# Attention beside a gated MLP on one core: the first token block's normalisation and gate/up matmuls rearranged, and the V tile's row cut from 136 to 129 elements

## The chip, the cores and the metric

The kernel runs on one core of a Trainium2 chip. The metric is the device time of one execution in microseconds (us). A core has a matmul engine (TensorE, PE in the profile; its weight loads are PEld), a vector engine (DVE), a scalar engine for activations (ACT), a general engine (POOL) and an engine that here only issues transfers (SP). They run side by side and wait for each other through semaphores; each works through its own instructions in order.

## The reference

```python
xn = layernorm(A_x)                               # 2048 x 512
q  = (xn @ wq) as 32 heads of 2048 x 128
p  = softmax(q @ k_cache^T * 128**-0.5)           # 2048 keys a head
s  = concat over heads(p @ v_cache) @ wo          # 2048 x 512
gate, up = xn @ W_gate, xn @ W_up                 # 2048 x 1792
g  = silu((relu(gate) * up) @ W_down)             # 2048 x 512
out = A_x + s * g
```

Everything is bf16 in memory; sums of products are float32.

## The kernel before, in words

The whole kernel is one program whose engine orders are written out by hand: each helper appends instructions to several engines' streams and returns a token (a semaphore and its count) that a later instruction waits for.

The 2048 tokens are 4 blocks (Q = 0 to 3) of 512 tokens, each of 4 tiles of 128. The first stage is the gated MLP. For each block the normalised tokens must stand transposed in `xnT` (features on the partitions). `emit_gate_up(Q)` (L462) makes 14 chunks (fc) of 128 hidden features: 4 matmuls of 512 columns with W_gate (L481) and 4 with W_up (L485), each group into one PSUM bank. Two banks are a slot of a ring of three slots (`ring_acquire`, L303), ps_r. ACT takes the relu of the gate bank (L448), DVE multiplies by the up bank (L454), which frees the slot. `emit_down(Q)` (L491) multiplies by W_down. While block 0's chunks run, DVE and ACT make the layer norm coefficients of the later blocks (`ln_task`, L416), POOL normalises those tiles (L340) and SP transposes them by DMA (L432).

Block 0 has no earlier work to hide behind; its path is the head, `head_ln` (L367). DVE takes the statistics of the tiles (L315, L320), ACT a square root (L326), DVE the reciprocal and a product (L331, L334) for tiles 0 and 1 together, and later for 2 and 3. All four tiles are normalised on DVE (`ln_norm`, L340), transposed on PE (`head_transpose`, L353) into PSUM tile ps_acc, and copied to `xnT` by ACT, the last by DVE (L359). PE runs 12 matmuls of zeros before (L365, `warm_mm`) and 3 more after the first two tiles' transposes. Then `emit_half(0, ...)` (L391) computes gate and up of the first three chunks (HFC = 3) for the first 256 tokens alone, as matmuls of 256 columns (L407), while tiles 2 and 3 are still being normalised; `emit_half(1, ...)` does the other 256 tokens. `emit_gate_up(0)` then only finishes these chunks, and goes on at full width from chunk 3.

The gate and up weights come in three pieces each, cut at the chunks FCS = 0, 3, 8, 14 (`load_w`, L220), all issued by SP; of the four x tiles of block 0 SP and ACT issue two each.

The second stage is attention, head by head, with blocks of 512 queries: scores (L625, 512 columns), exponential on ACT (L635), and the product with V (PV, L722): the exponentials are the stationary operand, and the moving operand is a row of `V_sb`, 128 values and a column of twos that gives the softmax denominator, so 129 columns. There are 8192 of these matmuls. `V_sb` has room for VS = 136 elements a row, of which 129 are used. V is loaded by SP, one transfer a head (L261), two heads ahead. `emit_norm_block` (L644) normalises a finished block and has SP transpose it by DMA (L661); the output projection of a group of four heads (L579) waits for the group's transposes.

Of the kernel before, what the change touches and what calls it, by code (L numbers as in the profile page):

```python
# [5 lines left out]
BF16 = mybir.dt.bfloat16  # L6
F32 = mybir.dt.float32
ALU = mybir.AluOpType
ACTF = mybir.ActivationFunctionType
# [42 lines left out]
def bass_recurrent_scan__mha_block_cached__glu_gated_reglu__prompt_kernel(  # L52
# [12 lines left out]
    _, S, D = A_x.shape  # L65
# [8 lines left out]
    DC = D // 128  # L74
# [13 lines left out]
    NBLK = H * QB  # L88
    TOTP = NBLK * NP
    VW = Dh + 1  # L90
    VS = Dh + 8
    TPG = 16 * G * QB

    x2 = A_x[0]
# [10 lines left out]
    with ExitStack() as es:  # L105
        _cnt = [0]

        def S_(shape, dt, name):
            _cnt[0] += 1
            return es.enter_context(nc.sbuf_tensor(f"{name}_{_cnt[0]}", shape, dt))  # L110
# [15 lines left out]
        ident = S_([128, 128], BF16, "ident")  # L126
        eps_sb = S_([128, 1], F32, "eps_sb")
        KT_sb = [S_([128, Sk], BF16, "KT_sb") for _ in range(2)]
        V_sb = [S_([128, KT, VS], BF16, "V_sb") for _ in range(2)]
        QT_sb = [S_([128, S], BF16, "QT_sb") for _ in range(2)]  # L130
        Wq_sb = [S_([128, DC, Dh], BF16, "Wq_sb") for _ in range(2)]
        Wo_sb = [S_([128, G, D], BF16, "Wo_sb") for _ in range(2)]
# [65 lines left out]
        with nc.Block() as block:  # L198

            @block.tensor  # L200
            def _(_pe_eng):
# [10 lines left out]
                for b in range(2):  # L212
                    tok_pool = sem_pool.sig(pool.memset(V_sb[b][:, :, Dh:VW], 2.0))

                FCS = [0, min(3, FC), min(8, FC), FC]
                HFC = 3
                wg_src = B_W_gate.rearrange("(c p) f -> p c f", p=128)
                wu_src = B_W_up.rearrange("(c p) f -> p c f", p=128)

# [18 lines left out]
                load_x0(sp, 2)  # L238
                load_x0(act, 3)
                load_w(sp, Wg_sb, wg_src, sem_wg, 0)  # L240
                load_w(sp, Wu_sb, wu_src, sem_wu, 0)
                load_w(sp, Wg_sb, wg_src, sem_wg, 1)
                load_w(sp, Wu_sb, wu_src, sem_wu, 1)
                if QB > 1:
# [98 lines left out]
                xt_ready = {Q: [] for Q in range(QB)}  # L343

                def head_transpose(n, ntok, eng, sem):
                    tp_ps = acc_bf[n % 2]
                    _wait(pe, acc_free[n % 2])
                    if n == 0:
                        _wait(pe, tok_pool)
                    _wait(pe, ntok)  # L350
                    ins = None
                    for c in range(DC):
                        ins = pe.transpose(tp_ps[:, c * 128:(c + 1) * 128],  # L353
                                           xn_sb[:, n, c * 128:(c + 1) * 128], ident[:])
                    ptok = sem_tp.sig(ins)
                    src = tp_ps[:, 0:DC * 128].rearrange("p (c q) -> p c q", c=DC)
                    _wait(eng, ptok)
                    copy = act.copy if eng is act else dve.tensor_copy
                    ctok = sem.sig(copy(xnT[:, :, n * 128:(n + 1) * 128], src))  # L359
                    xt_ready[0].append(ctok)  # L360
                    acc_free[n % 2] = ctok

                def warm_mm(k):
                    for _i in range(k):
                        pe.matmul(ps_r[:, 2 * NSLOT - 1, 0:D], warm[:, 0:128], warm[:], start=True, stop=True)  # L365

                def head_ln():  # L367
                    st = ln_stats(0)
                    st = ln_stats(1)
                    sq01 = ln_aggr([0, 1], st)  # L370
                    st = ln_stats(2)
                    c01 = ln_coef([0, 1], sq01)
                    n0 = ln_norm(dve, sem_ln4, 0, c01)
                    n1 = ln_norm(dve, sem_ln4, 1, c01)
                    head_transpose(0, n0, act, sem_xa)
                    head_transpose(1, n1, act, sem_xa)
                    warm_mm(3)
                    st = ln_stats(3)
                    sq23 = ln_aggr([2, 3], st)
                    emit_half(0, range(HFC - 1), xt_ready[0][0:2])  # L380
                    c23 = ln_coef([2, 3], sq23)
                    n2 = ln_norm(dve, sem_ln4, 2, c23)
                    n3 = ln_norm(dve, sem_ln4, 3, c23)
                    head_transpose(2, n2, act, sem_xa)
                    head_transpose(3, n3, dve, sem_xt)
                    emit_half(0, range(HFC - 1, HFC), [])
                    emit_half(1, range(HFC), xt_ready[0][2:4])

                half_slots = []

                def emit_half(k, fcs, toks):  # L391
                    hs = slice(k * 256, (k + 1) * 256)
                    for fc in fcs:
                        fs = slice(fc * 128, (fc + 1) * 128)
                        if k == 0:
                            if fc == 0:
                                pe.wait_ge(sem_wg[0].h, 16)
                            half_slots.append(ring_acquire())
                        if fc == 0:
                            _wait_all(pe, toks)  # L400
                        s = half_slots[fc]
                        for i, W in enumerate((Wg_sb, Wu_sb)):
                            if k == 0 and fc == 0 and i == 1:
                                pe.wait_ge(sem_wu[0].h, 16)
                            ins = None
                            for c in range(DC):
                                ins = pe.matmul(ps_r[:, 2 * s + i, hs], W[:, c, fs], xnT[:, c, hs],  # L407
                                                start=(c == 0), stop=(c == DC - 1))
                            if k == 1:
                                half_tok[(fc, i)] = (sem_gate if i == 0 else sem_gu).sig(ins)  # L410

                half_tok = {}

                ln_hold = {}

# [23 lines left out]
                sig_free = [None, None]  # L439
                hT_free = [None, None]  # L440

                def finish_gate_up(Q, fc, s, gtok, gu_tok):
                    par = Q % 2
                    gb = 2 * s
                    gk = fc % NSLOT
                    _wait(act, gtok)
                    _wait(act, gr_free[gk])
                    rtok = sem_relu.sig(act.activation(gr_sb[gk][:], ps_r[:, gb, :], ACTF.Relu))  # L448
                    _wait(dve, gu_tok)
                    _wait(dve, rtok)  # L450
                    if fc == 0:
                        _wait(dve, hT_free[par])
                    h_tok = sem_h.sig(
                        dve.tensor_tensor(hT[par][:, fc, :], gr_sb[gk][:], ps_r[:, gb + 1, :], ALU.mult)  # L454
                    )
                    gr_free[gk] = h_tok
                    ring_tok[s] = [rtok, h_tok]
                    if Q == 0:
                        ln_task(fc)
                    return h_tok  # L460

                def emit_gate_up(Q):  # L462
                    qs = slice(Q * NQ, (Q + 1) * NQ)
                    h_tok = None
                    for fc in range(FC):
                        fs = slice(fc * 128, (fc + 1) * 128)
                        if Q == 0 and fc < HFC:
                            s = half_slots[fc]
                            finish_gate_up(Q, fc, s, half_tok[(fc, 0)], half_tok[(fc, 1)])
                            continue  # L470
                        s = ring_acquire()
                        gb = 2 * s
                        if fc == 0:
                            _wait_all(pe, xt_ready[Q])
                        if Q == 0 and fc in FCS:
                            k = FCS.index(fc)
                            pe.wait_ge(sem_wg[k].h, 16)
                            pe.wait_ge(sem_wu[k].h, 16)
                        ins = None
                        for c in range(DC):  # L480
                            ins = pe.matmul(ps_r[:, gb, :], Wg_sb[:, c, fs], xnT[:, c, qs],  # L481
                                            start=(c == 0), stop=(c == DC - 1))
                        gtok = sem_gate.sig(ins)
                        for c in range(DC):
                            ins = pe.matmul(ps_r[:, gb + 1, :], Wu_sb[:, c, fs], xnT[:, c, qs],  # L485
                                            start=(c == 0), stop=(c == DC - 1))
                        gu_tok = sem_gu.sig(ins)
                        h_tok = finish_gate_up(Q, fc, s, gtok, gu_tok)
                    return h_tok

                def emit_down(Q, h_last_tok):  # L491
# [27 lines left out]

                assert DC == 4 and FC >= 4 * (QB - 1) + 1  # L520
                _wait(pe, warm_w)
                warm_mm(12)
                head_ln()
                for Q in range(QB):
                    hlast = emit_gate_up(Q)
                    if Q < QB - 1:
                        emit_down(Q, hlast)
# [177 lines left out]
                def emit_PV_tile(gp, tt):  # L705
# [11 lines left out]
                    for j in range(4):  # L717
                        bank = j // 2
                        if t == 0 and j % 2 == 0:
                            _wait(pe, norm_tok[b - 1][bank] if b >= 1 else acc_free[bank])  # L720
                        o_ap = ps_acc[:, bank, (j % 2) * 256:(j % 2) * 256 + VW]
                        ins = pe.matmul(o_ap, PT[pb][:, tt, j * 128:(j + 1) * 128], V_sb[vb][:, t, 0:VW],  # L722
                                        start=(t == 0 and j % 2 == 0), stop=(t == KT - 1 and j % 2 == 1))
                        if b == NBLK - 1 and t == KT - 1 and j == 1:
                            tx = sem_pv.sig(ins)
# [138 lines left out]
```

## Time and profile before

| | us |
|---|---|
| median of three runs | 1287.91 (1287.7 to 1288.04) |
| profiled execution, its own time | 1287.7 |
| its span, first to last instruction | 1285.8 |
| ACT's exponentials, L635, x1024 | 952.5 busy, 1054 ns each |
| scores, L625, 512 columns, x2048 | 754.1 busy, 379 ns each |
| gate and up at full width, L481 and L485, x212 each | 54.4 busy each, 379 ns each |
| V loads, L261, x32 | 512 KB each, 4.5 to landing |

The page gives an engine's busy time and, for a group of instructions, line, engine, operation, tiles, count, busy time and the mean duration of one. Matmuls are pipelined: the 379 ns of one with 512 columns is from its start to its modelled end, while the next starts 216 ns after it; so sums for PE go by the distances of starts, not by the durations. The chain of work that ended last follows back, from the last instruction, what each step waited for.

### The profile page before, as it was taken

To read this page: it belongs to the slowest core of one execution; us is meant where nothing else is said; L and a number is where in the kernel's file an instruction comes from. 1 tells how busy PE (TensorE), PEld (TensorE's weight loads), DVE (VectorE), ACT (ScalarE), POOL (GpSimd) and SP (SyncE) were. 2 spreads that over 40 slices of the span, in tenths; PEclk is the share of its full clock that TensorE was granted. 3 is DMA by queue.
4 is the path that set the end of the run, shared out by engine and by line. 5 is a ranking of instruction groups with operands and counts; after the bars stand their busy time and mean duration, and the time that the engine had idled before them with its cause. 6 is when DMAs were issued, how large, how long until landed. Compare 5 with 4: busy or idle time off the path is not lost.

```text
span 1285.8 us, 26847 instructions
## 1 busy us (share of the span) xinstructions
PE 1279.2 (99%) x11995; PEld 834.8 (65%) x11995; DVE 380.0 (30%) x682; ACT 1001.4 (78%) x1109; POOL 10.0 (1%) x21
## 2 busy tenths in 40 slices
PE   9999999999999999999999999999999999999998
PEld 4444476666666666666666666666666666666665
DVE  6333311112222222222222222222222222234456
ACT  3322399998888888888888888888888888888884
POOL 2000000000000000000000000000000000000000
PEclk9999999999999999999999999999999999999999
DMA  9500123232222332232322322332223321233302
GB/s 266 111 1 1 21 36 67 57 54 40 36 51 50 71 54 50 54 71 51 54 46 37 60 47 53 55 67 55 54 51 71 55 34 38 50 67 55 50 14 74
DMA packets 238801, 71.60 MB, mean 56 GB/s; under 512 B 225632, under 2 KB 238688, under 8 KB 238688
## 3 DMA queue, kind: packets, MB, share of 16 engines
q1 hardware_dynamic: 238400, 69.63, 27.8%
q8 instruction: 96, 1.57, 0.5%
q10 hardware_dynamic: 288, 0.26, 0.1%
q14 instruction: 17, 0.14, 0.0%
HBM read 32.77 MB, written 2.10 MB: 27 GB/s over the span
## 4 chain that ended last, share of the span: by engine, by line
PE 99%; DVE 1%; issue 0%; DMA 0%; ACT 0%
PE ps_acc L722 36%; PE ps_r L625 34%; PE ps_r L558 9%; PE ps_r L579 8%; PE ps_acc L504 4%; PE ps_r L485 4%; PE ps_r L481 4%; PE ps_r L759 1%; DVE fin_tmp L767 0%; PE ps_r L407 0%; DMA x_sb<-in_A_x_dram 0%; DVE stats L315 0%; ACT xnT L359 0%; PE ps_acc L353 0%; DVE x_sb L772 0%
## 5 line engine op out<-in xcount | busy, mean ns | idle before, releaser
L635 ACT ACTIVATE PT<-ps_r 128x1024 bf16<-128x1024 f32 x1024 | 952.5, 1054 | 167.7 <-PE ps_r L625 167.7
L722 PEld LDWEIGHTS ps_acc<-V_sb,PT 128*128 128x128 bf16 x8192 | 621.1, 98 | 241.7 <-ACT PT L635 3.5
L722 PE MATMUL ps_acc<-V_sb,PT 128*128 128x129 bf16 x8192 | 776.5, 220 | 0.0
L625 PE MATMUL ps_r<-QT_sb,KT_sb 128*128 128x512 bf16 x2048 | 754.1, 379 | 0.0
L652 DVE RECIPROCAL rz_sb<-ps_acc 128x4 f32<-128x4 f32 x127 | 23.3, 183 | 729.6 <-PE ps_acc L722 729.6
L625 PEld LDWEIGHTS ps_r<-QT_sb,KT_sb 128*128 128x128 bf16 x2048 | 195.0, 98 | 1.1 <-DVE QT_sb L569 0.4
L558 PE MATMUL ps_r<-xnT,Wq_sb 128*128 128x512 bf16 x512 | 130.9, 379 | 0.0
L579 PE MATMUL ps_r<-Wo_sb,OT_store 128*128 128x512 bf16 x448 | 114.6, 379 | 0.0
L569 DVE CAST QT_sb<-ps_r 128x512 bf16<-128x512 f32 x128 | 88.5, 692 | 48.1 <-PE ps_r L558 48.1
L558 PEld LDWEIGHTS ps_r<-xnT,Wq_sb 128*128 128x128 bf16 x512 | 49.9, 97 | 60.7 <-ACT PT L635 27.1
L655 DVE TENSOR_TENSOR Onorm<-ps_acc,rz_sb 128x512 bf16<-128x512 f32 x127 | 87.8, 691 | 4.4
L579 PEld LDWEIGHTS ps_r<-Wo_sb,OT_store 128*128 128x128 bf16 x448 | 43.8, 98 | 52.9 <-ACT PT L635 0.2
L448 ACT ACTIVATE gr_sb<-ps_r 128x512 bf16<-128x512 f32 x56 | 33.3, 596 | 51.5 <-PE ps_r L481 49.9
L592 DVE TENSOR_TENSOR s_acc<-s_acc,ps_r 128x512 f32<-128x512 f32 x96 | 66.0, 687 | 17.3 <-PE ps_r L579 17.3
L485 PE MATMUL ps_r<-xnT,Wu_sb 128*128 128x512 bf16 x212 | 54.4, 379 | 0.0
L481 PE MATMUL ps_r<-xnT,Wg_sb 128*128 128x512 bf16 x212 | 54.4, 379 | 0.0
L454 DVE TENSOR_TENSOR hT<-gr_sb,ps_r 128x512 bf16<-128x512 bf16 x56 | 38.4, 686 | 46.3 <-PE ps_r L485 42.0
L504 PE MATMUL ps_acc<-Wd_sb,hT 128*128 128x512 bf16 x224 | 49.0, 379 | 0.0
L510 ACT ACTIVATE sig_sb<-ps_acc 128x512 f32<-128x512 f32 x16 | 9.6, 597 | 38.8 <-PE ps_acc L504 38.8
L504 PEld LDWEIGHTS ps_acc<-Wd_sb,hT 128*128 128x128 bf16 x224 | 21.9, 98 | 26.4
L485 PEld LDWEIGHTS ps_r<-xnT,Wu_sb 128*128 128x128 bf16 x212 | 20.7, 98 | 25.0
L481 PEld LDWEIGHTS ps_r<-xnT,Wg_sb 128*128 128x128 bf16 x212 | 20.8, 98 | 24.8
(42 smaller groups left out, 138.7 us busy)
## 6 DMA issues: line engine op xcount, KB each, us to landing
V_sb<-in_A_v_cache_dram SPq DMA_DIRECT2D x32, 512.0 KB, 4.5
Wq_sb<-in_A_wq_dram SPq DMA_DIRECT2D x32, 128.0 KB, 2.4
Wo_sb<-in_A_wo_dram SPq DMA_DIRECT2D x8, 512.0 KB, 3.9
OT_store<-Onorm SPq DMA_TRANSPOSE x127, 2.4
Wd_sb<-in_B_W_down_dram SPq DMA_DIRECT2D x1, 1792.0 KB, 13.6
x_sb<-in_A_x_dram SPq DMA_DIRECT2D x3, 512.0 KB, 10.1
out_dram<-x_sb SPq DMA_DIRECT2D x6, 256.0 KB, 2.2
Wg_sb<-in_B_W_gate_dram SPq DMA_DIRECT2D x1, 768.0 KB, 9.8
```

The source lines that it names most:

```text
L454: dve.tensor_tensor(hT[par][:, fc, :], gr_sb[gk][:], ps_r[:, gb + 1, :], ALU.mult)
L481: ins = pe.matmul(ps_r[:, gb, :], Wg_sb[:, c, fs], xnT[:, c, qs], start=(c == 0), stop=(c == DC - 1))
L485: ins = pe.matmul(ps_r[:, gb + 1, :], Wu_sb[:, c, fs], xnT[:, c, qs], start=(c == 0), stop=(c == DC - 1))
L504: ins = pe.matmul(ps_acc[:, jb, 0:D], hT[par][:, fc, j * 128:(j + 1) * 128], Wd_sb[:, fc, :], start=(fc == 0), stop=(fc == FC - 1))
L558: ins = pe.matmul(ps_r[:, bank, :], Wq_sb[b][:, c, :], xnT[:, c, qs], start=(c == 0), stop=(c == DC - 1))
L569: etok = sem_qpe.sig(dve.tensor_copy(QT_sb[b][:, qs], ps_r[:, bank, :]))
L579: ins = pe.matmul(ps_r[:, bank, 0:D], OT_store[g % 2][:, hh, n * 128:(n + 1) * 128], Wo_sb[g % 2][:, hh, :], start=(hh == 0), stop=(hh == ...
L592: dve.tensor_tensor(s_acc[:, n, :], s_acc[:, n, :], ps_r[:, bank, 0:D], ALU.add)
L625: ins = pe.matmul(ps_r[:, 2 * s + tt, :], KT_sb[h % 2][:, t * 128:(t + 1) * 128], QT_sb[h % 2][:, qs], start=True, stop=True)
L635: act.activation(PT[pb][:], ps_r[:, 2 * s:2 * s + 2, :], ACTF.Exp, scale=scale)
L655: dve.tensor_tensor(Onorm[ob][:], o_ap, rz_sb[:].to_broadcast([128, 4, Dh]), ALU.mult))
L722: ins = pe.matmul(o_ap, PT[pb][:, tt, j * 128:(j + 1) * 128], V_sb[vb][:, t, 0:VW], start=(t == 0 and j % 2 == 0), stop=(t == KT - 1 and j ...
```

## The change

Two things change; the attention code itself doesn't, apart from the shape of V's tile.

1. The head of the kernel. Tiles 0 and 1 of block 0 are normalised by POOL instead of DVE, and DVE goes on with the statistics of tile 3. All four tiles' transposes on PE come after all normalisations in the program, and go into banks 0 to 3 of ps_r instead of ps_acc; the ring then starts at its third slot. The half-width matmuls of the first three chunks, and the 3 extra matmuls of zeros, go; chunks 0 to 2 are made at full width like the others. The first pieces of the gate and up weights hold 2 chunks instead of 3 (the second ones 6 instead of 5), and the first piece of W_up is issued by ACT.
2. `V_sb` has rows of 129 elements instead of 136, so a row starts 258 bytes after the one before instead of 272.

```diff
-    VS = Dh + 8
-        V_sb = [S_([128, KT, VS], BF16, "V_sb") for _ in range(2)]
+        V_sb = [S_([128, KT, VW], BF16, "V_sb") for _ in range(2)]
...
-                FCS = [0, min(3, FC), min(8, FC), FC]
-                HFC = 3
+                FCS = [0, min(2, FC), min(8, FC), FC]
...
-                load_w(sp, Wu_sb, wu_src, sem_wu, 0)
+                load_w(act, Wu_sb, wu_src, sem_wu, 0)
...
                 def head_transpose(n, ntok, eng, sem):
-                    tp_ps = acc_bf[n % 2]
-                    _wait(pe, acc_free[n % 2])
+                    tp_ps = ps_r[:, n, :].bitcast(BF16)
...
-                    acc_free[n % 2] = ctok
+                    ring_tok[n // 2].append(ctok)
...
                     c01 = ln_coef([0, 1], sq01)
-                    n0 = ln_norm(dve, sem_ln4, 0, c01)
-                    n1 = ln_norm(dve, sem_ln4, 1, c01)
-                    head_transpose(0, n0, act, sem_xa)
-                    head_transpose(1, n1, act, sem_xa)
-                    warm_mm(3)
+                    n0 = ln_norm(pool, sem_nm, 0, c01)
+                    n1 = ln_norm(pool, sem_nm, 1, c01)
                     st = ln_stats(3)
                     sq23 = ln_aggr([2, 3], st)
-                    emit_half(0, range(HFC - 1), xt_ready[0][0:2])
                     c23 = ln_coef([2, 3], sq23)
                     n2 = ln_norm(dve, sem_ln4, 2, c23)
                     n3 = ln_norm(dve, sem_ln4, 3, c23)
+                    head_transpose(0, n0, act, sem_xa)
+                    head_transpose(1, n1, act, sem_xa)
                     head_transpose(2, n2, act, sem_xa)
                     head_transpose(3, n3, dve, sem_xt)
-                    emit_half(0, range(HFC - 1, HFC), [])
-                    emit_half(1, range(HFC), xt_ready[0][2:4])
...
                     for fc in range(FC):
                         fs = slice(fc * 128, (fc + 1) * 128)
-                        if Q == 0 and fc < HFC:
-                            s = half_slots[fc]
-                            finish_gate_up(Q, fc, s, half_tok[(fc, 0)], half_tok[(fc, 1)])
-                            continue
                         s = ring_acquire()
...
-                warm_mm(12)
+                for _i in range(12):
+                    pe.matmul(ps_acc[:, 0, 0:D], warm[:, 0:128], warm[:], start=True, stop=True)
                 head_ln()
+                ring_cnt[0] = 2
...
-                        ins = pe.matmul(o_ap, PT[pb][:, tt, j * 128:(j + 1) * 128], V_sb[vb][:, t, 0:VW],
+                        ins = pe.matmul(o_ap, PT[pb][:, tt, j * 128:(j + 1) * 128], V_sb[vb][:, t, :],
```

Left out here: the functions `emit_half` and `warm_mm` are deleted, and `finish_gate_up` is written back into `emit_gate_up` unchanged.

## The prediction

> **What bounds the kernel now.** I read the page first, then the chain of work that ended last, then the timeline of the head, stage by stage.
>
> ```profile
> PE 1279.2 (99%) x11995; PEld 834.8 (65%) x11995; DVE 380.0 (30%) x682; ACT 1001.4 (78%) x1109; POOL 10.0 (1%) x21
> ...
> PE 99%; DVE 1%; issue 0%; DMA 0%; ACT 0%
> ...
> L722 PE MATMUL ps_acc<-V_sb,PT 128*128 128x129 bf16 x8192 | 776.5, 220 | 0.0
> ```
>
> TensorE carries 99% of the chain: from 7.80 us to the end it never waits long, so no other engine's work counts unless it makes PE late. An edit can therefore act in two places only: before PE's stream starts, and on the price of an instruction in the stream. The diff has one of each: a rewritten head, and a V row of 258 bytes (129 x 2) instead of 272 (136 x 2) under the 8192 matmuls of L722. (Normalisation and transposes of the attention blocks, L644 to L664, are untouched by the diff.)
>
> The chain, in order of time (start, length, what), shows what holds the head:
>
> ```profile
> 5.60 0.42 DVE xn_sb L340
> 6.02 0.14 issue
> 6.16 0.40 PE ps_acc L353 x4
> 6.55 0.02 issue
> 6.58 1.08 ACT xnT L359 x2
> 7.66 0.14 issue
> 7.80 1.91 PE ps_r L407 x16
> 9.70 0.45 PE ps_acc L353 x8
> 10.15 3.49 PE ps_r L407 x32
> ```
>
> Tiles 0 and 1 are normalised on DVE, transposed on PE and copied by ACT; at 7.80 the half-width gate/up matmuls (L407) start, tiles 2 and 3 are transposed in between (0.45 us), and 48 half matmuls cover chunks 0 to 2. The PE timeline (start, length) says when the full-width stream begins, and what came before:
>
> ```profile
> 1.19 4.25 PE L365 MATMUL ps_r<-warm 128*128 128x512 bf16 x12 [1.19 <-DVE warm L235]
> ...
> 13.48 1.03 PE L481 MATMUL ps_r<-xnT,Wg_sb 128*128 128x512 bf16 x4
> ```
>
> Chunk 3 starts at **13.48**. From there the instructions of both kernels are the same, so the head's effect is the shift of this one number.
>
> **The head, part by part.** Removed: 48 half matmuls (start to start 0.434 us for 4, so 5.2 us), the 3 warming matmuls at 6.62. Added: 24 full matmuls, 8 for each chunk. The timeline puts chunks 1.728 us apart (13.48, 15.21, 16.93), so three take 5.18 us: the matmul work is the same, but it may only start once all four tiles are transposed. Moved: tiles 0 and 1 go to POOL.
>
> ```profile
> L340 POOL TENSOR_SCALAR xn_sb<-x_sb,rstd,nmr x12: 767/768/769, 20.1 to 35.2; 128x512 bf16<-128x512 bf16 x12
> L340 DVE TENSOR_SCALAR xn_sb<-x_sb,rstd,nmr x4: 407/410/414, 5.6 to 8.6; 128x512 bf16<-128x512 bf16 x4
> ```
>
> (Each row: min/median/max ns.) Working forward from the coefficients, which end at 5.56 as before:
> - POOL: starts 0.10 after them (as at 20.00 to 20.11), tile 0 from 5.66 to 6.43, tile 1 to 7.18 (four took 3.01, a step of 0.75).
> - PE reacts 0.15 after a normalisation (6.01 to 6.16), the copy follows 0.42 after PE's start (6.16 to 6.58): transposes at 6.58 and 7.33, ACT copies 7.00 to 7.59 and 7.75 to 8.34.
> - DVE no longer normalises tiles 0 and 1 (0.74), so the statistics of tile 3 start at 5.57 instead of 6.25: 0.69, aggregates 0.25, end 6.53. ACT's square root 6.56 to 6.86 (it is ahead of the copies in ACT's order now; before it waited behind them until 7.54). Reciprocal at 6.89, product at 7.09, tile 2 normalised 7.28 to 7.69, tile 3 to 8.01.
> - Transposes at 7.84 and 8.16. ACT's third copy 8.26 to 8.84, DVE's copy of tile 3 from 8.59 (0.42) to 9.01.
> - PE starts gate/up 0.14 after the last copy (7.66 to 7.80): **9.15**. Chunk 3 then starts at 9.15 + 5.18 = 14.33 instead of 13.48: **+0.85 us**.
>
> ACT's chain has 0.17 us to spare against DVE's. If POOL and DVE slow each other (POOL's 767 to 769 ns held beside DVE's work at 20 us, but DVE's product with two SBUF inputs is at 7.09, while POOL ends tile 1), it is 0.1 to 0.3 us more; if the reactions are each a little faster, 0.2 less. So +0.6 to +1.3.
>
> Queues: SP loses one weight load and issues the rest 0.5 us earlier; ACT gains it behind its two x loads (0.89 us for both), 0.4 to 0.5 us, so its table load (1.28) ends at 3.4 and the dummy root at 3.6; its first real root came at 4.75. Hidden; without that cover it would cost 0.5. Weights: the first two chunks' loads shrink from 384 to 256 KB each and landed 4.6 and 5.6 us after issue, by 7.7, against 9.15. The next pieces grow to 768 KB, but the bytes up to the end of that piece are the same, and it landed at 3.22 + 8.1 = 11.3; chunk 2 needs it at 9.15 + 3.46 = 12.6. Hidden by 1.3 us. The transposes go to ps_r's banks 0 to 3, which the ring reuses at chunks 1 and 2, after the copies: nothing. DVE's first wait, the x load of tile 4, stands behind a product due at 11.1 and delays none that PE needs within a chunk.
>
> **The clock in the head.** What is lost with the warming matmuls and the early halves is PE's activity. Warming matmuls were 0.43 us apart at first and 0.216 later; the granted clock's record starts, at full, at 4.25. At the other end (PE busy, count, granted clock):
>
> ```profile
> 4.25:7.66 3.41, 2.47 (x17) 1.00 1.04 351
> 7.66:11.07 3.41, 3.27 (x34) 1.00 1.08 361
> ...
> 1280.83:1284.25 3.42, 1.11 (x6) 1.00 0.46 155
> ```
>
> ```profile
> 1284.30:1285.80 1.50, 0.00 (x0) 0.00 (x0) 0.00 (x0) 0.00 (x0) 0.00 (x0) 0.50 0.26 87
> ```
>
> A stretch with 2.47 us of PE kept the clock; after one with 1.11 it fell to half, 2.3 us after the last matmul's end. In the changed kernel the stretch 4.25 to 7.66 would hold 1.19 (rest of the warming) + 0.39 + 0.33 (two groups of transposes) = 1.9, between the two, nearer neither. If the clock falls there, gate/up starts at half speed and stays so until it rises: the start needed 3.06 us of matmuls (1.19 to 4.25), of which half is lost, **1.5 us**; it could be 1.0 if part of that has run off by 9.15, or 2.7 if the rise takes nearly twice as long. I take zero, since transposes count as PE work in these rows and no gap exceeds 1.2 us, but keep the rest for the range.
>
> The Trainium skill ("TensorE: Matmul & The Clock Gate", Why this matters for your kernels) says that no idle gap over some 3 us should stand between bursts, for one idle window brings half speed. By that rule alone this head is safe (sum +0.85), while the row at 1280.83, a stretch a third busy, speaks for a harsher rule (sum +2.4); the same page's Part 4 says that transposes don't count as PE-busy, which would make the gap 5.44 to 9.15, 3.7 us, and speaks against this change.
>
> **The V row.** Price of one PV matmul now:
>
> ```profile
> 1272.23 1.98 PE L722 MATMUL ps_acc<-V_sb,PT 128*128 128x129 bf16 x32
> ...
> 1274.04 3.62 PE L759 MATMUL ps_r<-Wo_sb,OT_store 128*128 128x512 bf16 x16
> ```
>
> 32 in 1.81 us are 56.6 ns each; a 512-column one is 216. So a column is (216 - 56.6)/383 = 0.416 ns and the fixed part 2.9 ns, for rows of 512 columns as for V's: the present rows show no penalty that a new stride could remove. No row shows a moving operand at a start that is no multiple of 4 or 16 bytes, so the cost is bounded: below, at most the fixed 2.9 ns (x 8192 = 24 us faster, which the equal fixed part of the wide rows speaks against); above, odd rows at half speed, 4096 x 53.7 ns = 220 us. The nearest row is the plain one, 0.416 ns a column, and 129 columns stay 129: zero. One column's time more in each would be 3.4 us.
>
> The Trainium skill ("SBUF — State Buffer", Door 1: The DMA port swizzle) says SBUF has 16-byte lines and that each crossing to a new line costs. It speaks against this change, but 258 bytes touch 17 lines from any even start, as they do now; by that rule the sum stays. No run here shows it.
>
> V's load writes 256-byte pieces at unaligned places. A load took 4.5 us to landing, with a whole head (35 us) of cover. The tight place is a group's last head: V issued at 285.65, the block's transpose behind it at 286.59, which lands within 5.4 us at most, and PE needs it at 294.69. 2.7 us are spare, 7 times: a load that takes 2.7 us more hides, one of twice the length leaves at most 1.8 us bare each time.
>
> **Sum.** The profiled execution took 1287.7 (span 1285.8, 1.9 around it); the median of the three runs is 1287.9, 0.2 above. Plus 0.85: 1288.6 beside the profiled one, **1288.8** against the median, +0.07%. A measurement of this kernel tells about 0.2% (2.6 us) from no change: above 1290.5 I count it slower, below 1285.3 faster.
>
> **Rivals.**
> 1. The clock falls in the head. For: 1.9 us is not far from 1.11. Against: four groups of transposes lie in the gap. +0.85 + 1.5 = +2.4, 1290.3 (1289.8 to 1291.5).
> 2. *Slower*: the misaligned V row costs each PV matmul time. Place L722, price 3.4 us for each column's time, so 1292.2 at one; it decides from (2.6 - 0.85)/8192 = 0.21 ns a matmul. For: PE has no slack there, every ns arrives. Against: the line count, and one column per cycle either way.
> 3. V's load takes twice as long and the groups' transposes come late: 7 x 1.8 = 12.6, 1301. Decides from 2.7 us more a load; against: no row shows a transfer slowed by its place.
> 4. PV gets cheaper, by 0.42 ns or more: 1285 or less. Nothing speaks for it but the bound.
> 5. The change doesn't do what it says: the head is as early as before (weights or x loads set it). The chain names copies, not loads: a part of the forecast's lower end.
>
> **How the numbers follow.** Forecast (head later, clock full, V free) 0.42, 1288.4 to 1289.3; clock falls 0.33, of which 0.11 above 1290.5; V row 0.18, two thirds of it near one column, the rest far above; late transposes 0.03; cheaper PV 0.04. Same: 0.42 + 0.22 = 0.64; slower: 0.11 + 0.18 + 0.03 = 0.32; faster 0.04. The range 1288.0 to 1292.5 holds the forecast, the clock's case and the V row at one column, and leaves out 0.06 + 0.03 + 0.04 = 0.13.
>
> **What would show it.** Head: POOL's first normalisation at 5.7, gate/up matmuls from 9.15, chunk 3 at 14.3. Clock: chunk 0's matmuls 0.216 apart, not 0.43, and no 0.50 in the granted clock before the end. V row: 32 PV matmuls in 1.81 us, and the stretch from the first PV to the last as long as now (159.5 to 1274.0, 1114.5). Loads: no wait of L579 on transposes. I am wrong if the stretch 159.5 to 1274.0 changes by more than 0.5 us, or if the shift at chunk 3 isn't the whole difference.

## The result and the profile after

The changed kernel takes **1292.36 us** (median of 4 runs, 1292.05 to 1293.98) against 1287.97 (4 runs, 1287.7 to 1288.06): ratio of the means 1.0037, 95% interval 1.002 to 1.0054. By the medians that is 4.4 us more, and slower by more than the 0.2% that the prediction set as its bound. The profiled executions differ by 4.6 (1292.28 and 1287.7), their spans by 4.5 (1290.3 and 1285.8). The forecast was no change.

Page of the changed kernel, busy time and the matmuls of PV (L679 now) and of the scores (L582):

```profile
PE 1282.7 (99%) x11968; PEld 835.2 (65%) x11968; DVE 379.3 (29%) x680; ACT 1001.6 (78%) x1109; POOL 11.5 (1%) x23
...
L679 PE MATMUL ps_acc<-V_sb,PT 128*128 128x129 bf16 x8192 | 780.5, 221 | 0.0
...
L582 PE MATMUL ps_r<-QT_sb,KT_sb 128*128 128x512 bf16 x2048 | 755.1, 380 | 0.0
```

The same 8192 PV matmuls are busy 780.5 us where they were 776.5, and the mean of one has gone from 220 to 221 ns; the scores gained 1.0 us. These are modelled durations of overlapping instructions, so they point at the place and do not price it. The head, PE's timeline (start, length):

```profile
1.19 4.34 PE L478 MATMUL ps_acc<-warm 128*128 128x512 bf16 x12 [1.19 <-DVE warm L233]
6.75 0.38 PE L350 MATMUL ps_r<-ident,xn_sb 128*128 128x128 bf16 x4 [1.22 <-POOL xn_sb L338]
7.41 1.18 PE L350 MATMUL ps_r<-ident,xn_sb 128*128 128x128 bf16 x12 [0.28 <-POOL xn_sb L338]
9.15 1.02 PE L422 MATMUL ps_r<-xnT,Wg_sb 128*128 128x512 bf16 x4 [0.56 <-DVE xnT L356]
...
14.32 1.03 PE L422 MATMUL ps_r<-xnT,Wg_sb 128*128 128x512 bf16 x4
```

Gate/up starts at 9.15, for which the prediction said 9.15, and chunk 3 at 14.32 (14.33): the head costs 14.32 - 13.48 = 0.84. The rest is in the stream. The line of the PV matmul, with first and last start, in the changed kernel:

```profile
L679 PE MATMUL ps_acc<-V_sb,PT x8192: 217/220/231, 160.3 to 1278.5; 128*128 128x129 bf16 x200
```

The same line in the kernel before:

```profile
L722 PE MATMUL ps_acc<-V_sb,PT x8192: 218/220/231, 159.5 to 1274.0; 128*128 128x129 bf16 x200
```

From the first PV to the last it is now 1118.2 us; before it was 1114.5. So 0.84 + 3.7 make the 4.5.

Which PV matmuls? The views round to 10 ns, but the starts in both traces, read one by one, give the distance from each matmul to the next. V's tile has 16 rows, each read by 4 matmuls in turn, with a score matmul behind every row from row 1 on; means over the 128 blocks, in ns:

| row of V | start of the row, bytes | before (272 a row) | after (258 a row) |
|---|---|---|---|
| 2, 4, ... 14 | multiple of 4 in both | 56.67 | 56.67 |
| 3, 5, ... 15 | after: 2 past a multiple of 4 | 56.67 | 56.7, then 57.5, 57.5, 57.5 |
| score matmul behind an odd row | | 215.83 | 216.67 |

Every matmul on an odd row costs **0.83 ns** more, two columns' time at the prediction's 0.416 each (called a tick below); it shows one interval late, so the first of a row has none and the score matmul behind the fourth has it. Even rows cost nothing, although most don't start at a multiple of 16. 4096 x 0.83 = 3.4 us. Row 1 is left out of the table: it is odd too, follows row 0 without a score matmul between, and with the score matmul behind it takes 5.2 ns more than before, where another odd row takes 3.3; 128 x 1.9 = 0.24 us (experiments 5 and 6 look at it). That makes 3.65. Summed over the trace, PV's intervals grew by 2.83 us and the scores' by 0.83: 3.66, with the head's 0.84 the whole 4.50.

### The profile page after: what moved, and what is told of

Same layout as the page of the kernel before. It is cut to its first block, busy times and chain, and to the rows that moved or that the text cites. A ratio compares the mean times of both kernels' runs of the same rounds, so it can differ in the third digit from the quotient of the medians.

```text
span 1290.3 us, 26792 instructions
## 1 busy us (share of the span) xinstructions
PE 1282.7 (99%) x11968; PEld 835.2 (65%) x11968; DVE 379.3 (29%) x680; ACT 1001.6 (78%) x1109; POOL 11.5 (1%) x23
## 4 chain that ended last, share of the span: by engine, by line
PE 98%; DVE 1%; issue 0%; DMA 0%; ACT 0%
PE ps_acc L679 36%; PE ps_r L582 34%; PE ps_r L515 9%; PE ps_r L536 7%; PE ps_r L422 4%; PE ps_r L426 4%; PE ps_acc L459 4%; PE ps_r L716 1%; DVE fin_tmp L724 0%; DMA x_sb<-in_A_x_dram 0%; DVE stats L313 0%; PE ps_r L350 0%; DVE x_sb L729 0%; DVE mv L318 0%; DVE Onorm L633 0%
## 5 line engine op out<-in xcount | busy, mean ns | idle before, releaser
L679 PE MATMUL ps_acc<-V_sb,PT 128*128 128x129 bf16 x8192 | 780.5, 221 | 0.0
L679 PEld LDWEIGHTS ps_acc<-V_sb,PT 128*128 128x128 bf16 x8192 | 622.9, 98 | 242.2 <-ACT PT L592 3.5
L582 PE MATMUL ps_r<-QT_sb,KT_sb 128*128 128x512 bf16 x2048 | 755.1, 380 | 0.0
L582 PEld LDWEIGHTS ps_r<-QT_sb,KT_sb 128*128 128x128 bf16 x2048 | 195.3, 98 | 1.1 <-DVE QT_sb L526 0.4
L515 PEld LDWEIGHTS ps_r<-xnT,Wq_sb 128*128 128x128 bf16 x512 | 49.8, 97 | 60.8 <-ACT PT L592 24.3
L422 PE MATMUL ps_r<-xnT,Wg_sb 128*128 128x512 bf16 x224 | 57.5, 379 | 0.6 <-DVE xnT L356 0.6
L426 PE MATMUL ps_r<-xnT,Wu_sb 128*128 128x512 bf16 x224 | 57.5, 379 | 0.0
```

The source lines that it names most:

```text
L515: ins = pe.matmul(ps_r[:, bank, :], Wq_sb[b][:, c, :], xnT[:, c, qs], start=(c == 0), stop=(c == DC - 1))
L582: ins = pe.matmul(ps_r[:, 2 * s + tt, :], KT_sb[h % 2][:, t * 128:(t + 1) * 128], QT_sb[h % 2][:, qs], start=True, stop=True)
```

## The experiments

**Theory:** a moving row that starts 2 bytes past a multiple of 4 costs each matmul one tick of 0.83 ns; the head costs its shift of chunk 3, more in runs where the clock falls in its gap. **Rivals:** the 16-byte lines; the transfers that write to odd places; the pitch or the tiles moved by the smaller tile; a head that costs more than it shows.

**1. Only the head** (a_row136): the changed kernel with padded rows.

```diff
+    VS = Dh + 8
...
-        V_sb = [S_([128, KT, VW], BF16, "V_sb") for _ in range(2)]
+        V_sb = [S_([128, KT, VS], BF16, "V_sb") for _ in range(2)]
...
-                        ins = pe.matmul(o_ap, PT[pb][:, tt, j * 128:(j + 1) * 128], V_sb[vb][:, t, :],
+                        ins = pe.matmul(o_ap, PT[pb][:, tt, j * 128:(j + 1) * 128], V_sb[vb][:, t, 0:VW],
```

> The changed kernel with V's rows of 136 elements again, so its new head alone. Theory (a matmul whose moving row starts 2 bytes past a multiple of 4 costs 0.83 ns more; 8 of the 16 rows of 258 bytes do, 4096 matmuls, 3.4 to 3.7 us; the head costs 0.85): 1288.8, i.e. 0.8 to 0.9 above the kernel before, and PV matmuls 56.67 ns apart on every row. Rival (the head costs more than its shift of chunk 3, and the row little): 1290 to 1292.

Measured 1288.9 (11 runs, 1288.42 to 1290.28) against 1287.99: 0.9 more, ratio 1.0008 (0.9999 to 1.0017). PV is 56.67 on every row. The interval touches 1, but no run of this kernel is below 1288.42 and none of the 23 of the one before above 1288.25; so the head costs about what the prediction said. But two of the 11 runs are at 1290.0 and 1290.3, and one of these was profiled. Stretches of its trace (length, PE's busy time and count, the granted clock, then the DMA's share and GB/s), and its timeline:

```profile
5.64:9.05 3.41, 1.99 (x18) 1.00 1.05 370
9.05:12.46 3.41, 3.40 (x9) 0.50 1.08 365
12.46:15.88 3.42, 3.42 (x17) 1.00 1.07 370
```

```profile
1.19 4.94 PE L479 MATMUL ps_acc<-warm 128*128 128x512 bf16 x12 [1.19 <-DVE warm L234]
...
9.06 1.86 PE L423 MATMUL ps_r<-xnT,Wg_sb 128*128 128x512 bf16 x4 [0.56 <-DVE xnT L357]
10.72 1.89 PE L427 MATMUL ps_r<-xnT,Wu_sb 128*128 128x512 bf16 x4
12.43 1.05 PE L423 MATMUL ps_r<-xnT,Wg_sb 128*128 128x512 bf16 x4
...
15.90 1.03 PE L423 MATMUL ps_r<-xnT,Wg_sb 128*128 128x512 bf16 x4
```

Here the clock came up later: its record begins, at full, at 5.64, where the changed kernel's begins at 4.42, and warming matmuls before that are 0.43 us apart. The 12 warming matmuls ended at 6.13, and in the gap behind them it fell to half at 9.05, for one stretch of 3.41 us. Chunk 0's matmuls are 0.42 us apart, chunk 3 starts at 15.90 instead of 14.32: 1.6 us. The prediction's first rival is real in single runs.

**2. Only the row** (b_row129): the kernel before with rows of 129.

```diff
-    VS = Dh + 8
+    VS = Dh + 1
```

> The kernel before with V's rows of 129 elements, nothing else. Theory (odd starts): 3.4 to 3.7 above the kernel before, 1291.5, with 57.5 ns on odd rows and 56.67 on even ones. Rival (the row costs only together with the new head, or nothing): 1288.0.

Measured 1291.5 (7 runs, 1291.4 to 1291.63): 3.5 more, ratio 1.0028 (1.0017 to 1.0039). 3.5 and 0.9 make the 4.4. Its rows show the same 56.67 and 57.5, and from its first PV matmul to its last it is 3.65 more.

**3. All rows odd** (b_odd_all): rows of 136, values and twos one element later.

```diff
-                    tok_pool = sem_pool.sig(pool.memset(V_sb[b][:, :, Dh:VW], 2.0))
+                    tok_pool = sem_pool.sig(pool.memset(V_sb[b][:, :, Dh + 1:VW + 1], 2.0))
...
-                    sem_v[b].sig(sp.dma_start(V_sb[b][:, :, 0:Dh], src))
+                    sem_v[b].sig(sp.dma_start(V_sb[b][:, :, 1:Dh + 1], src))
...
-                        ins = pe.matmul(o_ap, PT[pb][:, tt, j * 128:(j + 1) * 128], V_sb[vb][:, t, 0:VW],
+                        ins = pe.matmul(o_ap, PT[pb][:, tt, j * 128:(j + 1) * 128], V_sb[vb][:, t, 1:VW + 1],
```

> The kernel before with rows of 136 elements, but the values and the column of twos stored one element later, so that all 16 rows start 2 bytes past a multiple of 4. Theory (the start counts, not the pitch): 8192 x 0.83 = 6.8 above the kernel before, 1294.8. Rival (the odd pitch between rows costs, or the smaller tile that moves the tiles after it): 1288.0.

Measured 1294.63 (1294.56 to 1294.98): 6.6 more, ratio 1.0052 (1.0038 to 1.0066), nearly twice the row's cost from twice the matmuls; from its first PV matmul to its last it is 6.8 more, 0.83 for each of the 8192. The PV line of this kernel's page:

```profile
L722 PE MATMUL ps_acc<-V_sb,PT 128*128 128x129 bf16 x8192 | 784.0, 222 | 0.0
```

222 where half odd rows gave 221 and none 220. The pitch is that of before, and so are the places of the other tiles: the start counts.

**4. Odd writes, even reads** (b_odd_load): the column of twos first, the values after it.

```diff
-                    tok_pool = sem_pool.sig(pool.memset(V_sb[b][:, :, Dh:VW], 2.0))
+                    tok_pool = sem_pool.sig(pool.memset(V_sb[b][:, :, 0:1], 2.0))
...
-                    sem_v[b].sig(sp.dma_start(V_sb[b][:, :, 0:Dh], src))
+                    sem_v[b].sig(sp.dma_start(V_sb[b][:, :, 1:Dh + 1], src))
...
-                    return v[:, :, 0:Dh], v[:, :, Dh:Dh + 1]
+                    return v[:, :, 1:Dh + 1], v[:, :, 0:1]
```

> The kernel before with the column of twos first and the values after it, rows of 136: the transfers write 2 bytes past a multiple of 4, TensorE reads 129 columns from a multiple of 16. Theory (TensorE's read of the row costs): 1288.0, as before. Rival (the transfers' writes to odd places slow TensorE or come late): 1291 to 1295.

Measured 1287.95, ratio 1.0 (0.9991 to 1.0009): nothing. The transfers do take longer, 5.2 us instead of 4.5 (4.5 to 4.8 in the traces of the kernels whose V rows are written from multiples of 4 bytes); issued two attention heads ahead, they stay hidden. This kernel's V loads, with the median from issue to landing last:

```profile
V_sb<-in_A_v_cache_dram SPq DMA_DIRECT2D x32, 512.0 KB, 5.2
```

**5. A multiple of 4, not of 16** (b_row130): `VS = Dh + 2`.

> The kernel before with V's rows of 130 elements: 260 bytes, so every row starts at a multiple of 4, but 12 of 16 rows at no multiple of 16. Theory (only a start 2 past a multiple of 4 costs): 1288.0, as before. Rival (lines of 16 bytes, or any padding less than 16 bytes): 1290 to 1293.

Measured 1288.3 (1288.14 to 1288.42) against 1287.97: ratio 1.0002 (0.9993 to 1.0011). The rival that a start off a 16-byte line costs is out: 12 of 16 rows off a line would have cost as the odd rows did. 0.3 us are left; rows 2 to 15 show no step, but the first matmul of row 1, which follows row 0's last with no score matmul between, takes 60.8 ns, and the four of that row 1.7 more than elsewhere, 128 x 1.7 = 0.2 us.

**6. What that first matmul is** (b_row140): `VS = Dh + 12`.

> The kernel before with rows of 140 elements: 280 bytes, a multiple of 8 but not of 16; row 1 starts 22 bytes after row 0's last value, no longer within 16. It asks about the 0.3 us of the rows of 130, where the first matmul of row 1 took 60.8 ns. Theory (that matmul is slow because row 1 starts in the 16 bytes in which row 0 ends): 56.67 ns there, 1288.0. Rival (because row 1 doesn't start at a multiple of 16): 60.8 ns there again, 1288.3.

Measured 1288.02 (1287.9 to 1288.09), as before; the matmul took 59.2, between the two, and gave all of it back within the row (59.2 + 55.8 + 55.8 + 55.8). Neither expectation met it: the time agrees with the first, the slow matmul is nearer the second. It stays open, and is worth 0.3 us at most.

**7. One column more** (b_cols130): `VW = Dh + 2`, rows of 136.

> The kernel before with 130 columns a PV matmul (two columns of twos; the second one's sums aren't used). Theory (TensorE takes columns in pairs of 0.83 ns, so 129 cost as 130): 1288.0, PV 56.67 ns apart. Rival (each column 0.416 ns, and the tick on odd starts is something else): 8192 x 0.416 = 3.4 more, 1291.4.

Measured 1288.03, ratio 1.0 (0.9991 to 1.0009): the 130th column is free.

**8. One column less** (b_cols128): `VW = Dh`, the twos in the last value column's place. This kernel leaves the last value column of each head out of the output, so it serves as a measurement alone.

> The kernel before with 128 columns a PV matmul: the column of twos stands in the place of the last value column, so the last of the 128 value columns of each head is left out of the output. Theory (columns in pairs: 129 cost 65 pairs, 128 cost 64): 8192 x 0.83 = 6.8 less, 1281.2, PV 55.83 ns apart. Rival (0.416 ns a column): 3.4 less, 1284.6.

Measured 1281.31 (1281.23 to 1281.67): 6.7 less, ratio 0.9949 (0.9933 to 0.9964). The PV line of its page:

```profile
L722 PE MATMUL ps_acc<-V_sb,PT 128*128 128x128 bf16 x8192 | 769.4, 219 | 10.8
```

From the first PV matmul to the last it is 1107.7 us, 6.8 less. The distance from one to the next is 55.84 ns against 56.67. So here the price goes by twos of columns: 64 ticks of 0.83 ns for 128, 65 for 129 and for 130, and 2.5 ns for each matmul; 256 ticks and 2.5 ns give the 215.83 of 512 columns too.

**9. A wide moving operand** (b_qt_odd): the query tile one element later, 2048 matmuls of 512 columns.

```diff
-        QT_sb = [S_([128, S], BF16, "QT_sb") for _ in range(2)]
+        QT_sb = [S_([128, S + 16], BF16, "QT_sb")[:, 1:S + 1] for _ in range(2)]
```

> The kernel before with the query tile, the moving operand of the 2048 score matmuls of 512 columns, stored one element later, so that all of them start 2 bytes past a multiple of 4. Theory (one tick of 0.83 ns a matmul, whatever its width): 2048 x 0.83 = 1.7 more, 1289.7. Rival 1 (one for each pair of columns): 440 more. Rival 2 (it is peculiar to the 129 columns, an odd start with an odd count): 1288.0.

Measured 1289.82 (1289.58 to 1289.97): 1.85 more, ratio 1.0014 (1.0005 to 1.0023), 0.9 ns a matmul; in the trace the stretch from the first PV to the last, which holds the score matmuls, grew by 1.7 us, 0.83 for each. One tick for each instruction, at 512 columns as at 129. Why is open: 512 columns from an odd start touch one aligned pair of elements more than from an even one (257 for 256), but 129 touch 65 either way and pay the tick too, so counting the pairs touched doesn't explain it.

**10. Work in the head's gap** (a_row136_warm): two matmuls of zeros after the first and two after the second tile's transposes.

> The new head with rows of 136 and four more matmuls of zeros in its gap, two after the first and two after the second tile's transposes, which use no time that the path has. Theory (the runs of a_row136 at 1290.0 to 1290.3 are those in which the clock fell in the gap): 1288.8 with no run above 1289.4. Rival (these runs have another cause, such as when the loads land): the same spread, 1288.4 to 1290.3.

Measured 1288.89 (11 runs, 1288.69 to 1289.94): ten runs up to 1289.04, one at 1289.94. No run was to be above 1289.4, and one is; one late run of 11 instead of two says little either way: inconclusive.

**11. Little work before** (a_row136_cold): 4 warming matmuls at the start instead of 12.

> The new head with rows of 136 and 4 warming matmuls at the start instead of 12, so that TensorE has little to do before the gate and up matmuls at 9.1. Theory (the runs of a_row136 at 1290 are those with the clock at half when these matmuls start): nearly every run starts them at half speed, for one to two stretches of 3.41 us less what has run off, so 1.0 to 3.4 above 1288.8, the median near 1291, and the profile shows 0.43 us between chunk 0's matmuls. Rival (the warming is of no use to this head, its spread has another cause): 1288.4 to 1290.3 as before.

Measured 1290.09 (11 runs, 1289.71 to 1291.54) against 1287.94, ratio 1.0018 (1.0009 to 1.0027); every run is above all but two of a_row136's. The median is 0.9 lower than expected. Its timeline:

```profile
9.58 1.86 PE L423 MATMUL ps_r<-xnT,Wg_sb 128*128 128x512 bf16 x4 [0.56 <-DVE xnT L357]
11.24 1.91 PE L427 MATMUL ps_r<-xnT,Wu_sb 128*128 128x512 bf16 x4
12.95 1.27 PE L423 MATMUL ps_r<-xnT,Wg_sb 128*128 128x512 bf16 x4
...
16.64 1.03 PE L423 MATMUL ps_r<-xnT,Wg_sb 128*128 128x512 bf16 x4
```

Half speed, by the 0.42 us between matmuls, until some way into chunk 1 (12.95), where the clock's record begins, at full, at 13.43; chunk 3 at 16.64: 2.3 us behind the changed kernel's. The 8 warming matmuls more are worth 1.2 us in the median.

**12. A shorter head** (b_st2_late): the kernel before with the statistics of tile 2 after the normalisation of tiles 0 and 1.

> The kernel before with the statistics of tile 2 after the normalisation of tiles 0 and 1 on DVE, not between their aggregates and their reciprocal. Theory (the head's chain is the whole of what the head costs, and these statistics hold DVE to 5.30 where the root ends at 5.05): up to 0.2 less, 1287.8. Rival (tiles 2 and 3 become late by the 0.6 that is moved, and PE waits for them): 1288.0 to 1288.5.

Measured 1287.92 against 1288.01, ratio 0.9999 (0.999 to 1.0008): no difference. In its trace gate/up starts at 7.85, no earlier than before; there the warming matmuls, at half speed for longer, ended only at 6.24 and held the transposes. No kernel that computes the reference beats the one before by a difference that these runs can tell.

## Why the prediction was wrong

- **The head: right in its order and its sum.** 0.85 forecast, 0.84 in the trace and 0.9 alone (experiment 1). POOL's tiles, the order on DVE and the last copy (predicted 9.01, it ended at 9.05) came as worked out. That 9.15 was met to the hundredth is in part luck: the x tiles landed 0.17 later than before, and quicker reactions made up for it. The first weight loads, though smaller, took longer than worked out (the last landed at 8.4, not by 7.7), still ahead of 9.15.
- **The clock: the size was right, the yes or no was not one.** Taken as zero, which is true of the profiled execution; two of the other three runs lie beside it. In a profiled run of the same head the clock did fall, for 1.6 us (1.5 predicted), after a stretch with 1.99 us of PE, most of it transposes. So the ground for zero, that transposes count as PE work, doesn't hold as it stands, and the zero was in part luck. The fourth run of the changed kernel, 1293.98, lies 1.7 above the others; it has no trace, so that this was the clock is argued, not shown.
- **The V row: the step that failed.** "129 columns stay 129: zero." The trace had no row with an odd start, and zero was chosen since the nearest row has a price by the column. But the price goes by pairs of columns, and an odd start adds one more tick: 0.83 ns for 4096 matmuls and 0.24 us at row 1, 3.65 us in the trace and 3.5 as a run's time (experiment 2). The second rival (3.4 us, 1292.2) is what happened, with a chance of 0.18. Its bound of one column's time for each of 8192 matmuls came out right by luck: it is two columns' time for half of them. The point from which it decides, 0.21 ns a matmul, should have told that a price this small can't be excluded by an argument about whole columns.
- The Trainium skill's rule ("SBUF — State Buffer", Door 1) has lines of 16 bytes; by it the sum stayed. Experiment 5 and the even rows show no cost for starts off 16 bytes where they are multiples of 4, and the odd rows cost although, by the prediction's count, they touch no line more; so the rule's unit isn't the one that decided here.
- **Loads, late transposes, a cheaper PV: right, none came.** V's load grew from 4.5 to 4.9 us, far from the 2.7 to spare.
- **The fixed part: a circle.** One slope and one fixed part were drawn through two widths, 129 and 512, and then the equal fixed part was called evidence that V's rows pay nothing extra. Two points always lie on one line. With a third width (experiments 7 and 8) it is 2.5 ns and 0.83 for each pair; 129 columns pay for 130, and the 0.4 ns between 2.9 and 2.5 was the missing half of a pair.

## What to carry to other kernels

Where TensorE is the bound, start every row of a bf16 moving operand at a multiple of 4 bytes and count its columns by twos: a row pitch of an odd number of elements costs the matmuls on every second row 0.83 ns each, which is 0.3% here and grows with the share of short matmuls. Padding the row to an even pitch was enough to within 0.3 us. In a head that waits on other engines, look at what TensorE does in its gaps: a gap can cost more by the clock than by its length, and not in each run.

## What the runs showed of the hardware

- From one matmul to the next at the full clock: 55.84 ns for 128 columns, 56.67 for 129 and 130, 57.5 for 129 from an odd start; 215.83 for 512, and 0.83 more from an odd start.
- Transfers of 256-byte pieces to odd places took 5.2 instead of 4.5 to 4.8 us to landing for 512 KB, and did not slow TensorE (experiment 4).
- The clock's record has steps of 3.41 us: 5.64, 9.05, 12.46 in one trace. PE's busy time doesn't decide it alone: 1.99 us in the stretch before it fell (0.49 of warming and 16 transposes), while this stretch of the changed kernel, with 1.11 of warming and 8 transposes, kept it:

```profile
4.42:7.83 3.41, 1.89 (x13) 1.00 1.01 323
```

So transposes seem to count for less than matmuls. The Trainium skill ("TensorE: Matmul & The Clock Gate", Part 4) says that they don't count as PE work in the same way, which agrees; its advice to avoid idle gaps over some 3 us (Why this matters for your kernels) did not cover this gap, 2.9 us between matmuls with transposes in it.
